# Linear attention and a leaky-ReLU MLP: the state's update in one VectorE operation, the decayed k in a tile of its own, another order of the first units, two raw weight buffers

## The chip, the cores and the metric

The kernel runs on one core of a Trainium2 chip. The metric is the device time of one execution in microseconds (us). Before the change the median of three runs is 626.47 us (625.44 to 629.3).

TensorE multiplies matrices into PSUM. VectorE (DVE in the profile), ScalarE (ACT) and GpSimd (POOL) work element by element; the SP engine only issues transfers here. Each engine works off its own instructions in order, and waits where an instruction needs another engine's result.

## What is computed

For 4 batches, 8 heads, 768 positions and 64 channels per head, an attention with decay goes through blocks of 64 positions and carries one 64x64 state per head. Its output is the input x of a two-layer network:

```python
for b in range(nb):                       # nb = 768 / 64 = 12 blocks
    intra = einsum('bhic,bhjc->bhij', qb, kb) * Dmask[None]
    intra = einsum('bhij,bhjd->bhid', intra, vb)
    inter = einsum('bhid,bhde->bhie', qb * lam_pow[None], kv_state)
    out[:, :, sl] = intra + inter
    kb_dec = kb * rev_pow[None]
    kv_state = lam_block * kv_state + einsum('bhsd,bhse->bhde', kb_dec, vb)
...
h = x @ w_in                              # x: 3072 x 512, w_in: 512 x 2048
g = maximum(0.01 * h, h)
return g @ w_out                          # w_out: 2048 x 512
```

The weights come as 64-bit floating-point numbers; everything else is 32-bit.

## The kernel before

**Chunks.** The attention is worked in 24 chunks of 128 positions, six per batch, each of two blocks. Chunk c has these stages:

- `load_kq`, `load_v`: five transfers on SP's queue into one of two sets of buffers `kqv`.
- `transposes`: four TensorE transposes of k (line 331, for the first four chunks into the PSUM bank named by `KT`, later into `po`) and four of q (into `pt`); then copies on ScalarE (lines 340, 341), the decay of k in place on GpSimd (line 345; VectorE is allowed for the first chunk, `KM`), and the scaled q on GpSimd (line 349, from the copy of q; for chunks below `QS` it would be VectorE, from PSUM).
- `scores`: the state products `kv` of decayed k and v, and the scores `go`, both on TensorE into the PSUM tile `psc` (line 286); then on VectorE the scores times the decay (line 375), and for each of the two blocks an addition of the state product to a state that has already been multiplied by the decay of a block (line 382, or a copy at a batch's start, line 380). After each block GpSimd writes the decayed state into the next of four state tiles (line 385), to which the next block adds.
- `outputs`: TensorE makes the output in `po` from scores and v (`own`) and from state and scaled q (`inter`, twice); ScalarE and VectorE split it into three fp32r terms xh, xl, xm (lines 430, 431, 433), the left operand of the network.

**Groups and units.** Four chunks make a group of 512 tokens, so there are six groups. `w_in` has eight weight pairs p of 256 columns. For each half of a pair, `to_float32` loads 512 KB into one of `NRAW` buffers `raw` (line 485, on ScalarE's queue; for the output weights line 488, on SP's), reads it three times with ScalarE (lines 497, 499, 501) and makes 32-bit numbers with VectorE (lines 503, 504). `parts` then splits the pair into wh, wl, wm (lines 510 or 512, 515, 521). `up(g, p, lo, hi)` is a unit: the product of group g's chunks lo to hi with pair p. For each of two column blocks f it has three products (h, l, m) of four matmuls each (line 561), ScalarE passes between them (lines 579, 582) and a store of the result to DRAM (line 585). Its PSUM banks `b10`, `b11`, `b2` go round; the first `EARLY` blocks leave out `b11`. A unit can be cut into pieces of fewer chunks, which then go as separate units.

**Down.** From 360 us on, `down` multiplies the stored results, split again into three terms, with `w_out` (line 620), whose weights pass through `raw` and DRAM during the groups before. The last `raw` buffer also holds the temporary `tt` of the final additions.

**The order.** `seq` at line 658 is a list written out by hand for groups 0 and 1: "a" is a whole chunk alone, "b" begins two chunks, "r" is a round (outputs of c, scores of c + 1, transposes of c + 2), "wi" a weight pair, "up" a unit. The class `Plan` collects all operations with an assumed engine and duration and the tiles they read and write. `emit` then lays them out, always taking what can start earliest, and among equals the lower place in `seq`; each engine's instructions are issued in that order. Where the plan expects TensorE to be idle, `busy` puts placeholder transposes (line 253) into a bank that is not used yet (`spare`); they end with the first unit that uses this bank.

```python
seq = [("a", 0), ("a", 1), ("a", 2), ("a", 3), ("wi", 1), ("b", 4), ("wi", 0), ("up", 0, 1), ("up", 0, 0), ("wi", 2),
```

The `att` tile holds all the attention's buffers (8608 words per partition); each `raw` buffer has 1024.

Of the kernel before, what the change touches and what calls it, by code (L numbers as in the profile page):

```python
# [36 lines left out]
class Plan:  # L37
# [2 lines left out]


    LAG = {"PE": 0.25, "ACT": 0.1, "DVE": 0.1, "POOL": 0.12, "DMA": 3.5}
    SOON = dict(LAG, DMA=2.0)

    def __init__(self):
        self.ops, self.last, self.rank = [], {}, 0.0
        self.chain, self.chains = None, {}
        self.warm = 0.0
        self.first = {"PE": 0.0, "ACT": 0.0, "DVE": 3.4, "POOL": 0.0, "DMA": 0.2}
        self.cold, self.idle, self.spare = 6.0, None, None  # L50

    def begin(self, name):
# [28 lines left out]
    def emit(self):  # L81
        n = len(self.ops)
        follows, heads = {}, {}
        for c in self.chains.values():
            m = [i for i in c if "PE" in self.ops[i][0]]
            for i in c[1:]:
                self.ops[m[0]][2].update(self.ops[i][2] - set(c))
            heads[m[0]] = m[1:]
            follows.update((i, m[0]) for i in m[1:])
        locked = []  # L90
        left = [len(o[2]) for o in self.ops]
        users = [[] for _ in range(n)]
        for i, o in enumerate(self.ops):
            for d in o[2]:
                users[d].append(i)
        free = dict(self.first)
        ends = [[] for _ in range(n)]
        able = {e: set() for e in free}
        for i, o in enumerate(self.ops):
            if not left[i]:  # L100
                for e in o[0]:
                    able[e].add(i)

        def since(i, e):
            return max((t + (0.0 if e == x != "DMA" else self.LAG[x]) for t, x in ends[i]), default=0.0)

        def good(i, e, t):
            ways = self.ops[i][0]
            return all(t + ways[e] <= max(free[x], t) + ways[x] + 0.3 for x in ways)

        done = []
        while len(done) < n:
            best = None
            for e in free:
                for i in able[e]:
                    if e == "PE" and (i != locked[0] if locked else i in follows):
                        continue
# [12 lines left out]
            if e == "PE" and t < self.cold:  # L130
                us *= 1.5
            elif e == "DVE" and fn is not None and free["POOL"] > t:
                us += 0.4 * min(free["POOL"] - t, us)
            free[e] = t + us
            done.append((t, len(done), i, e))
# [9 lines left out]
        soon.update(PE=self.warm, DVE=self.first["DVE"], DMA=self.first["DMA"])  # L145
        over = [(0.0, None)] * n
        for t, _, i, e in self.timeline:
            ways, fn, deps = self.ops[i][:3]
            t = max([soon[e]] + [over[d][0] + (0.0 if over[d][1] == e != "DMA" else self.SOON[over[d][1]]) for d in deps])
# [11 lines left out]
def kernel(  # L161
# [10 lines left out]
    nc = tc.nc  # L172
# [11 lines left out]
    T = GC * C  # L184
    WARM = 9
    LATER = 4.0
    KT, EARLY = "b11", 1
    QS = 0
    KM = 1
    NRAW = 3  # L190
    HALF = (slice(0, D), slice(D, 2 * D))
    assert D == 64 and KO == HP == 4 and SEQ % C == 0 and NCH % GC == 0 and d_model == T == 512 and NP % 4 == 0

# [29 lines left out]
    NA = 8608  # L223
    att = sb([P, NA], "att")
    used = 0

# [4 lines left out]
        return att[:, used - n:used]  # L231

    ident = part(P)
    kqv = [[part(H * D).rearrange("p (h d) -> p h d", h=H) for _ in range(2)] for _ in range(3)]
    kTs, qTs, qsTs = ([part(HP * C).rearrange("p (y t) -> p y t", y=HP) for _ in range(2)] for _ in range(3))
    sc = part(2 * HP * C2).rearrange("p (x y t) -> p x y t", x=2, y=HP)
# [13 lines left out]
    def busy(n):  # L250

        for _ in range(n):
            nc.tensor.transpose(out=b1[0][:, 0:P], in_=ident, identity=ident)  # L253

    busy(WARM)
    nc.gpsimd.memset(zero, 0.0)
    plan = Plan()
    plan.idle, plan.spare, plan.warm = busy, "b10", 1.3 + 0.22 * WARM
    add = plan.add

    def factors_k():
# [42 lines left out]
    def load_kq(c):  # L304
        b, n, i = of(c)
        for src, x, nm in ((k, 0, "k"), (q, 1, "q")):
            y, dst = src[b, :, n * C:(n + 1) * C, :], kqv[x][i]

            def go(y=y, dst=dst):
                for z in range(2):  # L310
                    nc.sync.dma_start(out=dst[:, z * HP:(z + 1) * HP, :], in_=y[z::2].rearrange("h p d -> p h d"))  # L311
            add("DMA", 1.15, go, [], [f"{nm}{i}"])

    def load_v(c):
        b, n, i = of(c)
        add("DMA", 1.15, lambda: nc.sync.dma_start(out=kqv[2][i], in_=v[b, :, n * C:(n + 1) * C, :].rearrange("h p d -> p h d")),
            [], [f"v{i}"])

    def transposes(c):
# [16 lines left out]
        def copies():  # L336
# [5 lines left out]
            kr = tk.rearrange("p (y x) d -> p y x d", x=2)  # L342
            nr = slice(0, C2 if n == NCB - 1 else P)
            add(*((("DVE", "POOL"), (0.7, 1.1)) if c < KM else ("POOL", 1.1)),
                lambda e="POOL": ENG[e].tensor_tensor(kr[nr], kr[nr], _bc(pow_k, 3, D)[nr], op=ALU.mult), ["fk"], [f"k{i}"])  # L345
            m = slice(1 if n == 0 else 0, 2)
            o, x = (z.rearrange("p y (t i) -> p y t i", t=2)[:, :, m, :] for z in (qsTs[i], pt if c < QS else qTs[i]))
            eng, e, us, dep = ("DVE", nc.vector, 0.7, "pt") if c < QS else ("POOL", nc.gpsimd, 1.2, f"qT{i}")
# [1 line left out]

        return copies

    def scores(c):
        b, n, i = of(c)
        tk, tv, kT, qT = kqv[0][i], kqv[2][i], kTs[i], qTs[i]
        n_pu = 1 if n == NCB - 1 else 2

        def go():
# [9 lines left out]
                        h = y // 2 + (2 * y + x) % HP * 2  # L368
                        quad(pu[t][:, y, :], t, tk[:, 2 * y + x, :], tv[:, h, :], x, start=y == 0)

        add("PE", 0.47, kv, [f"k{i}", f"v{i}"], ["psc"])
        add("PE", 0.47, go, [f"kT{i}", f"qT{i}"], ["psc"])

        def uses():
            add("DVE", 0.69, lambda: nc.vector.tensor_tensor(sc, psc[:, :, lower, :], decay, op=ALU.mult), ["psc", "fk"], ["sc"])  # L375
            for t in range(n_pu):
                j = 2 * c + t
                new = state[j % 4]
                if n == 0 and t == 0:
                    add("DVE", 0.42, lambda new=new: nc.vector.tensor_copy(new, pu[0]), ["psc"], [f"st{j % 4}"])  # L380
                else:
                    add("DVE", 0.42, lambda new=new, t=t: nc.vector.tensor_tensor(new, new, pu[t], op=ALU.add),  # L382
                        ["psc"], [f"st{j % 4}"])
                if n_pu == 2:
                    add("POOL", 0.7, lambda new=new, j=j: nc.gpsimd.tensor_tensor(state[(j + 1) % 4], new, _bc(lam_c, 2, D), op=ALU.mult),  # L385
                        [f"st{j % 4}", "fq"], [f"st{(j + 1) % 4}"])

        return uses

# [48 lines left out]
    def alone(c):  # L438
        load_kq(c)
        load_v(c)  # L440
        transposes(c)()
        scores(c)()
        outputs(c)()

    def begun(c):

        for x in (c, c + 1):
            load_kq(x)
            load_v(x)
            transposes(x)()  # L450
        scores(c)()

    def round_of(c):

# [11 lines left out]
        for x in after:  # L466
            x()
        if c + 2 < NCH:
            load_v(c + 2)


# [3 lines left out]
    def to_float32(kind, p, h, dst, key, after=()):  # L475
# [17 lines left out]
        def addend(dt, i):  # L493
            return low.bitcast(dt).rearrange("p (n two) -> p n two", two=2)[:, :, i]

        add("DMA", 1.6, load, after, [f"raw{j}"])
        add("ACT", 0.67, lambda: nc.scalar.activation(out=dst, in_=words(1, F32), func=AF.Abs, scale=2.0 ** -110),
            [f"raw{j}"], [key])
        add("ACT", 0.78, lambda: nc.scalar.activation(out=addend(U16, 0), in_=words(0, U32), func=AF.Copy, bias=0.0, scale=2.0 ** -29),
# [28 lines left out]
            to_float32("wi", p, h, w32[:, h, :], f"w32{h}")  # L528
        parts(p, w32f, ["w320", "w321"])

    ATT = ["fk", "fq", "sc"] + [f"{x}{i}" for x in ("k", "q", "v", "kT", "qT", "qsT") for i in range(2)] + [f"st{i}" for i in range(4)]
    NR = 4
    graw = [att[:, j * 2 * T:(j + 1) * 2 * T] for j in range(NR)]

# [73 lines left out]
    def down(g, p):  # L608

        nonlocal n_t  # L610
        for tb in range(GC):
# [43 lines left out]

    seq = [("a", 0), ("a", 1), ("a", 2), ("a", 3), ("wi", 1), ("b", 4), ("wi", 0), ("up", 0, 1), ("up", 0, 0), ("wi", 2),
# [77 lines left out]
```

## Time and profile before

| | us |
|---|---|
| median of three runs | 626.47 |
| the profiled execution's own time | 626.15 |
| its span | 623.6 |
| TensorE busy | 613.9 |
| its weight loads busy | 513.5 |
| VectorE busy | 297.9 |
| ScalarE busy | 281.2 |
| GpSimd busy | 91.7 |

The span is what the profile covers; 2.55 us of the execution lie around it. The page's second part cuts the span into 40 slices of 15.6 us; a digit is the busy share in tenths:

```profile
PE   8899999999999999999999999999999999999997
DVE  4799882400344333333145763735545454535531
ACT  3688875443577766664444722312222222314111
POOL 4852513300332222222000000000000000000000
DMA  9998844632787778842455762432524333333201
```

One reads a column from top to bottom: which engines were busy at the same time. In the list of groups, a row gives line, engine, operation, output and inputs with their shapes, how often, then the total busy us, the mean ns of one, and the idle time of the engine just before them with what ended it. In the timeline a row gives the start, the length, the engine and the line.

### The profile page before, as it was taken

The page shows a single profiled execution, that of the slowest core. Times are in us where ns is not written, and L with a number is a line of the kernel's source. Part 1 is how long each engine was busy: PE and PEld are TensorE (multiplying, and loading weights), DVE is VectorE, ACT ScalarE, POOL GpSimd, SP SyncE. Part 2 cuts the span into 40 slices and gives each one's busy share as a digit, 9 for nine tenths or more (in the row PEclk, how much of TensorE's full clock was granted, in tenths as well). Part 3 has the DMA queues.
Part 4 walks back from the last instruction along what each step waited for, and adds up shares of the span by engine and source line. Part 5 has one row for each costly group of instructions (what it writes and reads, how often), then busy time and mean ns, then how long its engine had stood idle before and what let it go on. Part 6 is the DMA issues. An engine that isn't in the chain of part 4 may idle for free.

```text
span 623.6 us, 13157 instructions
## 1 busy us (share of the span) xinstructions
PE 613.9 (98%) x5578; PEld 513.5 (82%) x5578; DVE 297.9 (48%) x366; ACT 281.2 (45%) x461; POOL 91.7 (15%) x95
## 2 busy tenths in 40 slices
PE   8899999999999999999999999999999999999997
PEld 7688888898888888888788888888888888888885
DVE  4799882400344333333145763735545454535531
ACT  3688875443577766664444722312222222314111
POOL 4852513300332222222000000000000000000000
PEclk9999999999999999999999999999999999999999
DMA  9998844632787778842455762432524333333201
GB/s 201 250 259 259 243 156 136 155 111 91 206 248 253 245 238 259 247 163 87 169 202 189 247 203 72 153 117 82 188 67 135 136 106 131 128 109 118 85 0 67
DMA packets 103706, 101.51 MB, mean 163 GB/s; under 512 B 78560, under 2 KB 80608, under 8 KB 103648
## 3 DMA queue, kind: packets, MB, share of 16 engines
q1 hardware_dynamic: 99152, 92.29, 47.3%
q10 hardware_dynamic: 4496, 8.39, 4.3%
q8 instruction: 43, 0.70, 0.5%
q14 instruction: 15, 0.12, 0.1%
HBM read 65.02 MB, written 35.65 MB: 161 GB/s over the span
## 4 chain that ended last, share of the span: by engine, by line
PE 96%; DMA 2%; SPq 0%; POOL 0%; DVE 0%; ACT 0%; issue 0%; DVEq 0%
PE b L561 43%; PE b L620 17%; PE po L620 11%; PE psc L620 10%; PE po L286 4%; PE pt L620 3%; PE psc L286 3%; PE po L331 2%; PE pt L331 2%; DMA att<-in_q_dram 2%; PE b L253 1%; DMA att<-in_k_dram 1%; SPq L311 0%; PE b L331 0%; POOL att L345 0%
## 5 line engine op out<-in xcount | busy, mean ns | idle before, releaser
L602 ACT ACTIVATE xh<-att 128x1024 fp32r<-128x1024 f32 x48 | 50.9, 1061 | 147.3 <-PE po L620 141.3
L603 DVE SCALAR_TENSOR_TENSOR xl<-att,xh 128x1024 fp32r<-128x1024 f32 x48 | 58.7, 1223 | 99.4 <-ACT xh L602 99.4
L561 PE MATMUL b<-xh,wh 128*128 128x512 f32 (+3 forms) x416 | 105.5, 377 | 0.0
L561 PE MATMUL b<-xl,wl 128*128 128x512 f32 (+3 forms) x416 | 105.4, 376 | 0.0
L561 PE MATMUL b<-xm,wm 128*128 128x512 f32 (+3 forms) x416 | 104.9, 381 | 0.0
L561 PEld LDWEIGHTS b<-xl,wl 128*128 128x128 f32 x416 | 75.5, 188 | 14.7 <-DVE wl L515 0.2
L561 PEld LDWEIGHTS b<-xh,wh 128*128 128x128 f32 x416 | 75.3, 188 | 14.3
L561 PEld LDWEIGHTS b<-xm,wm 128*128 128x128 f32 x416 | 73.5, 188 | 13.2
L579 ACT ACTIVATE b<-b 128x512 f32<-128x512 f32 (+2 forms) x98 | 56.7, 579 | 57.1 <-PE b L561 56.3
L582 ACT ACTIVATE gs<-b 128x512 f32<-128x512 f32 (+2 forms) x98 | 57.8, 590 | 48.7 <-PE b L561 40.2
L375 DVE TENSOR_TENSOR att<-psc,att 128x512 f32<-128x512 f32 x24 | 16.5, 688 | 128.3 <-PE psc L286 128.2
L620 PE MATMUL b<-wl,xl 128*128 128x512 f32 x192 | 74.7, 389 | 0.0
L620 PE MATMUL b<-wh,xh 128*128 128x512 f32 x192 | 74.7, 389 | 0.0
L605 DVE SCALAR_TENSOR_TENSOR xm<-xl,xh 128x1024 fp32r<-128x1024 f32 x48 | 58.8, 1226 | 4.8
L345 POOL TENSOR_TENSOR att<-att 128x512 f32<-128x512 f32 (+1 forms) x24 | 27.6, 1149 | 141.1 <-PE po L331 133.5
L620 PEld LDWEIGHTS b<-wh,xh 128*128 128x128 f32 x192 | 36.1, 188 | 7.5
L620 PEld LDWEIGHTS b<-wl,xl 128*128 128x128 f32 x192 | 36.0, 188 | 7.5
L385 POOL TENSOR_TENSOR att<-att 128x256 f32<-128x256 f32 x40 | 35.6, 889 | 28.7 <-DVE att L382 23.4
L620 PE MATMUL po<-wm,xm 128*128 128x512 f32 (+1 forms) x100 | 37.2, 381 | 0.7 <-ACT raw L642 0.7
L620 PE MATMUL psc<-wh,xh 128*128 128x512 f32 x96 | 37.4, 389 | 0.0
L620 PE MATMUL po<-wl,xl 128*128 128x512 f32 x96 | 37.4, 389 | 0.0
L620 PE MATMUL b<-wm,xm 128*128 128x512 f32 x96 | 37.4, 389 | 0.0
(67 smaller groups left out, 817.1 us busy)
## 6 DMA issues: line engine op xcount, KB each, us to landing
att<-g SPq DMA_DIRECT2D x48, 512.0 KB, 3.2
g<-gs SPq DMA_DIRECT2D x45, 512.0 KB, 2.9
raw<-in_moe_w_in_dram ACTq DMA_DIRECT2D x16, 512.0 KB, 5.0
raw<-in_moe_w_out_dram SPq DMA_DIRECT2D x16, 512.0 KB, 4.3
att<-in_k_dram SPq DMA_DIRECT2D x48, 128.0 KB, 4.0
att<-in_q_dram SPq DMA_DIRECT2D x48, 128.0 KB, 3.7
att<-in_v_dram SPq DMA_DIRECT2D x24, 256.0 KB, 3.9
out_dram<-gs SPq DMA_DIRECT2D x23, 256.0 KB, 2.2
```

Source lines behind the costliest of these rows:

```text
L286: nc.tensor.matmul(dst[HALF[cols]], lhsT=lhsT[HALF[rows]], rhs=rhs[HALF[rows]], start=start, stop=True, skip_group_check=True)
L331: nc.tensor.transpose(out=at[y], in_=src[:, 2 * y:2 * y + 2, :].rearrange("p a d -> p (a d)"), identity=ident)
L345: lambda e="POOL": ENG[e].tensor_tensor(kr[nr], kr[nr], _bc(pow_k, 3, D)[nr], op=ALU.mult), ["fk"], [f"k{i}"])
L375: add("DVE", 0.69, lambda: nc.vector.tensor_tensor(sc, psc[:, :, lower, :], decay, op=ALU.mult), ["psc", "fk"], ["sc"])
L385: add("POOL", 0.7, lambda new=new, j=j: nc.gpsimd.tensor_tensor(state[(j + 1) % 4], new, _bc(lam_c, 2, D), op=ALU.mult), [f"st{j % 4}", "f ...
L561: nc.tensor.matmul(dst, lhsT=w[z][:, kk * 2 * P + f * P:kk * 2 * P + (f + 1) * P], rhs=x[z][:, kk, toks], start=start and kk == 0, stop=kk ...
L579: add("ACT", ns, lambda b=b: nc.scalar.activation(out=b, in_=b, func=AF.Copy, bias=0.0, scale=S + 1.0), [], [kb], rank=-1.5)
L582: add("ACT", ns, lambda b=b, r=r: nc.scalar.activation(out=r, in_=b, func=AF.Prelu, bias=0.0, scale=1.0 / WS, alpha=0.01), [kb], [f"gs{jg} ...
L602: add("ACT", 1.05, lambda: nc.scalar.activation(out=h, in_=graw[j], func=AF.Copy, bias=0.0, scale=NEAR), reads, wr("h"))
L603: add("DVE", 1.25, lambda: nc.vector.scalar_tensor_tensor(l, graw[j], 1.0, h.bitcast(F32), op0=ALU.mult, op1=ALU.subtract), reads + [f"rh{ ...
L605: add("DVE", 1.25, lambda: nc.vector.scalar_tensor_tensor(m, l.bitcast(F32), -S, h.bitcast(F32), op0=ALU.mult, op1=ALU.add), [f"rh{j}", f" ...
L620: nc.tensor.matmul(acc[tb][z // 2][:, cols], lhsT=ring[j][z][:, f * T + tb * P:f * T + (tb + 1) * P], rhs=W[pp][z][:, f * d_model:(f + 1) ...
```

## The change

- **State.** The GpSimd product at line 385 and the addition at line 382 are replaced by `scalar_tensor_tensor` on VectorE: new state = old state times the decay, plus the state product from PSUM. The factor is one number per partition and head pair, so an update is four instructions of 128x64.
- **Decayed k.** It goes into a tile `k_dec` of its own, one for all chunks, in a new stage `decayed(c)`, which the units "a", "b" and "r" call; the state products read `k_dec`.
- **Order.** `seq` for groups 0 and 1 is another list. Pair 1 comes after chunk 1, pair 0 after chunk 3; units cut into pieces are now 1 and 2 of group 0 (two halves each) and 7 of group 1 (three chunks and one).
- **Banks.** k's first transposes use `b10`, placeholders `b11`, and two early blocks leave out `b11`. The scaled q of chunks 0 and 1 is VectorE's, from PSUM (`QS` = 2).
- **Buffers.** `raw` has two buffers in place of three; `att` grows by 512 words.
- **Planning.** The plan names the loads of `w_in` an engine "WDMA" of its own, which it lets share time with "DMA", and some assumed durations differ. These add no instruction.

```diff
-    KT, EARLY = "b11", 1
-    QS = 0
+    KT, EARLY = "b10", 2
+    SPARE = "b11" if KT == "b10" else "b10"
+    QS = 2
     KM = 1
-    NRAW = 3
+    NRAW = 2
...
+    k_dec = part(H * D).rearrange("p (h d) -> p h d", h=H)
...
-            nc.tensor.transpose(out=b1[0][:, 0:P], in_=ident, identity=ident)
+            nc.tensor.transpose(out=bank[SPARE][:, 0:P], in_=ident, identity=ident)
...
-            add(*((("DVE", "POOL"), (0.7, 1.1)) if c < KM else ("POOL", 1.1)),
-                lambda e="POOL": ENG[e].tensor_tensor(kr[nr], kr[nr], _bc(pow_k, 3, D)[nr], op=ALU.mult), ["fk"], [f"k{i}"])
...
+    def decayed(c):
+        b, n, i = of(c)
+        nr = slice(0, C2 if n == NCB - 1 else P)
+        kr, kd = (z.rearrange("p (y x) d -> p y x d", x=2)[nr] for z in (kqv[0][i], k_dec))
+        add(*((("DVE", "POOL"), (0.7, 1.1)) if c < KM else ("POOL", 1.1)),
+            lambda e="POOL": ENG[e].tensor_tensor(kd, kr, _bc(pow_k, 3, D)[nr], op=ALU.mult), ["fk", f"k{i}"], ["kd"])
...
-        add("PE", 0.47, kv, [f"k{i}", f"v{i}"], ["psc"])
+        add("PE", 0.47, kv, ["kd", f"v{i}"], ["psc"])
...
-                new = state[j % 4]
+                new, old = state[j % 4], state[(j - 1) % 4]
+
+                def update(new=new, old=old, t=t):
+                    for y in range(HP):
+                        nc.vector.scalar_tensor_tensor(new[:, y, :], old[:, y, :], lam_c[:, y:y + 1], pu[t][:, y, :],
+                                                       op0=ALU.mult, op1=ALU.add)
...
-                    add("DVE", 0.42, lambda new=new, t=t: nc.vector.tensor_tensor(new, new, pu[t], op=ALU.add),
-                        ["psc"], [f"st{j % 4}"])
-                if n_pu == 2:
-                    add("POOL", 0.7, lambda new=new, j=j: nc.gpsimd.tensor_tensor(state[(j + 1) % 4], new, _bc(lam_c, 2, D), op=ALU.mult),
-                        [f"st{j % 4}", "fq"], [f"st{(j + 1) % 4}"])
+                    add("DVE", 0.55, update, ["psc", "fq", f"st{(j - 1) % 4}"], [f"st{j % 4}"])
...
         transposes(c)()
+        decayed(c)
         scores(c)()
...
+        decayed(c)
         scores(c)()
+        decayed(c + 1)
...
         if c + 2 < NCH:
+            decayed(c + 2)
             load_v(c + 2)
...
-        add("DMA", 1.6, load, after, [f"raw{j}"])
+        add("WDMA" if kind == "wi" else "DMA", 1.65, load, after, [f"raw{j}"])
...
-    seq = [("a", 0), ("a", 1), ("a", 2), ("a", 3), ("wi", 1), ("b", 4), ("wi", 0), ("up", 0, 1), ("up", 0, 0), ("wi", 2),
-           ("r", 4), ("wi", 3), ("up", 0, 2), ("up", 0, 3), ("r", 5), ("r", 6), ("r", 7), ("wi", 7), ("up", 1, 3, 0, 1),
-           ("wi", 4), ("up", 1, 1, 0, 2), ("wi", 6), ("up", 0, 7), ("up", 0, 4), ("up", 1, 7, 1, 3), ("up", 0, 6),
-           ("wi", 5), ("up", 0, 5), ("up", 1, 5), ("r", 8), ("r", 9), ("r", 10), ("up", 1, 7, 3, 4), ("r", 11),
-           ("up", 1, 2), ("up", 1, 0), ("up", 1, 7, 0, 1), ("up", 1, 3, 1, 4), ("up", 1, 1, 2, 4), ("up", 1, 6),
-           ("up", 1, 4)]
+    seq = [("a", 0), ("a", 1), ("wi", 1), ("a", 2), ("a", 3), ("wi", 0), ("up", 0, 1, 0, 2), ("b", 4), ("wi", 2), ("r", 4),
+           ("wi", 3), ("up", 0, 0), ("up", 0, 1, 2, 4), ("up", 0, 2, 0, 2), ("up", 0, 2, 2, 4), ("up", 0, 3), ("r", 5),
+           ("wi", 7), ("wi", 6), ("up", 0, 7), ("r", 6), ("up", 1, 7, 0, 3), ("up", 0, 6), ("wi", 4), ("r", 7), ("wi", 5),
+           ("up", 0, 4), ("up", 1, 6), ("up", 0, 5), ("r", 8), ("up", 1, 3), ("r", 9), ("up", 1, 5), ("up", 1, 7, 3, 4),
+           ("r", 10), ("up", 1, 0), ("r", 11), ("up", 1, 4), ("up", 1, 2), ("up", 1, 1)]
```

More of the change, by code (lines that the diff above doesn't have):

```diff
@@ L42 @@
     LAG = {"PE": 0.25, "ACT": 0.1, "DVE": 0.1, "POOL": 0.12, "DMA": 3.5}
-    SOON = dict(LAG, DMA=2.0)
+    LAG["WDMA"] = LAG["DMA"]
+    SOON = dict(LAG, DMA=2.0, WDMA=2.0)
+    LOADS = ("DMA", "WDMA")
     def __init__(self):
@@ L48, in __init__ @@
         self.warm = 0.0
-        self.first = {"PE": 0.0, "ACT": 0.0, "DVE": 3.4, "POOL": 0.0, "DMA": 0.2}
+        self.first = {"PE": 0.0, "ACT": 0.0, "DVE": 3.4, "POOL": 0.0, "DMA": 0.2, "WDMA": 0.2}
         self.cold, self.idle, self.spare = 6.0, None, None
@@ L104, in since @@
         def since(i, e):
-            return max((t + (0.0 if e == x != "DMA" else self.LAG[x]) for t, x in ends[i]), default=0.0)
+            return max((t + (0.0 if e == x and x not in self.LOADS else self.LAG[x]) for t, x in ends[i]), default=0.0)
         def good(i, e, t):
@@ L134, in emit @@
             free[e] = t + us
+            if e in self.LOADS:
+                free.update(dict.fromkeys(self.LOADS, t + us))
             done.append((t, len(done), i, e))
@@ L144, in emit @@
         soon = dict.fromkeys(free, 0.0)
-        soon.update(PE=self.warm, DVE=self.first["DVE"], DMA=self.first["DMA"])
+        soon.update(self.first, PE=self.warm)
         over = [(0.0, None)] * n
@@ L148, in emit @@
             ways, fn, deps = self.ops[i][:3]
-            t = max([soon[e]] + [over[d][0] + (0.0 if over[d][1] == e != "DMA" else self.SOON[over[d][1]]) for d in deps])
+            t = max([soon[e]] + [over[d][0] + (0.0 if over[d][1] == e and e not in self.LOADS else self.SOON[over[d][1]]) for d in deps])
             if e == "PE":
@@ L220 @@
     G = [[dram.tile([P, 2 * T], F32, name=f"g{g}_{p}", tag=f"g{g}_{p}") for p in range(NP)] for g in range(NG)]
-    NA = 8608
+    NA = 8608 + 512
     att = sb([P, NA], "att")
@@ L257 @@
     plan = Plan()
-    plan.idle, plan.spare, plan.warm = busy, "b10", 1.3 + 0.22 * WARM
+    plan.idle, plan.spare, plan.warm = busy, SPARE, 1.3 + 0.22 * WARM
     add = plan.add
@@ L311, in go @@
                     nc.sync.dma_start(out=dst[:, z * HP:(z + 1) * HP, :], in_=y[z::2].rearrange("h p d -> p h d"))
-            add("DMA", 1.15, go, [], [f"{nm}{i}"])
+            add("DMA", 1.2, go, [], [f"{nm}{i}"])
     def load_v(c):
         b, n, i = of(c)
-        add("DMA", 1.15, lambda: nc.sync.dma_start(out=kqv[2][i], in_=v[b, :, n * C:(n + 1) * C, :].rearrange("h p d -> p h d")),
+        add("DMA", 1.2, lambda: nc.sync.dma_start(out=kqv[2][i], in_=v[b, :, n * C:(n + 1) * C, :].rearrange("h p d -> p h d")),
             [], [f"v{i}"])
@@ L341, in copies @@
             add("ACT", 0.6, lambda: nc.scalar.copy(qTs[i], pt), ["pt"], [f"qT{i}"])
-            kr = tk.rearrange("p (y x) d -> p y x d", x=2)
-            nr = slice(0, C2 if n == NCB - 1 else P)
-            add(*((("DVE", "POOL"), (0.7, 1.1)) if c < KM else ("POOL", 1.1)),
-                lambda e="POOL": ENG[e].tensor_tensor(kr[nr], kr[nr], _bc(pow_k, 3, D)[nr], op=ALU.mult), ["fk"], [f"k{i}"])
             m = slice(1 if n == 0 else 0, 2)
@@ L351, in transposes @@
         return copies
+    def decayed(c):
[4 more added lines that the diff above has]
+            lambda e="POOL": ENG[e].tensor_tensor(kd, kr, _bc(pow_k, 3, D)[nr], op=ALU.mult), ["fk", f"k{i}"], ["kd"])
     def scores(c):
         b, n, i = of(c)
-        tk, tv, kT, qT = kqv[0][i], kqv[2][i], kTs[i], qTs[i]
+        tk, tv, kT, qT = k_dec, kqv[2][i], kTs[i], qTs[i]
         n_pu = 1 if n == NCB - 1 else 2
@@ L529, in w_in @@
         parts(p, w32f, ["w320", "w321"])
-    ATT = ["fk", "fq", "sc"] + [f"{x}{i}" for x in ("k", "q", "v", "kT", "qT", "qsT") for i in range(2)] + [f"st{i}" for i in range(4)]
+    ATT = ["fk", "fq", "sc", "kd"] + [f"{x}{i}" for x in ("k", "q", "v", "kT", "qT", "qsT") for i in range(2)] + [f"st{i}" for i in range(4)]
     NR = 4
```

## The prediction

> **What bounds the kernel now.** I read the busy shares first, then the chain of waits, then the busy times by stretch, then the timeline of the first 70 us. TensorE is busy 98% of the span and its weight loads 82%; the chain that ended last is TensorE almost throughout:
>
> ```profile
> PE 96%; DMA 2%; SPq 0%; POOL 0%; DVE 0%; ACT 0%; issue 0%; DVEq 0%
> ```
>
> So an edit counts only where it removes work from TensorE or closes a hole in it. The stretches show where holes are; the columns after the length are TensorE matmuls, its weight loads, VectorE, ScalarE and GpSimd, each in busy us, then the clock, the DMA share and GB/s:
>
> ```profile
> 0.00:30.00 30.00, 24.92 (x576) 20.07 (x577) 18.37 (x42) 15.63 (x28) 18.72 (x24) 1.00 0.99 224
> 30.00:60.00 30.00, 30.00 (x426) 24.93 (x425) 28.43 (x37) 25.58 (x45) 11.87 (x11) 1.00 0.93 264
> 60.00:90.00 30.00, 30.00 (x394) 26.56 (x394) 25.75 (x38) 24.59 (x44) 11.65 (x10) 1.00 0.71 210
> 125.00:310.00 185.00, 184.72 (x2180) 155.82 (x2180) 55.60 (x89) 111.49 (x204) 38.01 (x40) 1.00 0.60 192
> ```
>
> Only the first 30 us have holes: 5.1 us idle, and beside it the placeholder transposes of line 253, which compute nothing. From 30 us on TensorE has none; but VectorE is busy 28.43 of 30 us between 30 and 60, so it is nearly a second bound there. From 125 us VectorE is 30% busy. Groups of instructions and one line of the waits (us in total, times, longest):
>
> ```profile
> L253 PE MATMUL b<-att 128*128 128x128 f32 x38 | 8.4, 349 | 1.4 <-POOL att L256 1.4
> L382 DVE TENSOR_TENSOR att<-att,psc 128x256 f32<-128x256 f32 x40 | 16.5, 412 | 5.0 <-POOL att L385 5.0
> L385 POOL TENSOR_TENSOR att<-att 128x256 f32<-128x256 f32 x40 | 35.6, 889 | 28.7 <-DVE att L382 23.4 <-DVE att L380 4.7 <-DMA att<-in_k_dram 0.5
> DVE att L382 <- POOL att L385: 5.0, 5, 2.2
> ```
>
> TensorE's removable start is thus at most 5.1 + 8.4 = 13.5 us; some 4 us of it, until the first k lands at 4.0, no order of the units touches. The timeline gives the dates that matter (start, length, engine):
>
> ```profile
> 10.00 0.38 ACTq L485 DMA_DIRECT2D raw<-in_moe_w_in_dram  x1
> ...
> 14.61 0.37 ACTq L485 DMA_DIRECT2D raw<-in_moe_w_in_dram  x1
> ...
> 26.27 1.22 DVE L515 SCALAR_TENSOR_TENSOR wl<-wh,w 128x1024 fp32r<-128x1024 f32 x1
> ...
> 29.46 2.12 PE L561 MATMUL b<-xh,wh 128*128 128x512 f32 x8
> ```
>
> The two halves of the first weight pair are asked for at 10.0 and 14.6, and the first weight product runs at 29.46. Later pairs come just in time: the l part of pair 2 is made at 45.60 to 46.83 while TensorE starts that unit at 46.01, that of pair 3 at 53.96 to 56.27 for a unit begun at 54.68. VectorE, in order, makes them.
>
> [...] Trace: line 512 takes 1.44 us at 35.28 beside GpSimd's line 345, 0.69 alone; line 382, one input in PSUM, never left 0.40 to 0.42. The new update has one SBUF tensor and one PSUM tensor, so I expect it undisturbed.
>
> **Part by part.**
>
> *State update.* Removed: 40 GpSimd products (35.6 us), and 40 VectorE additions of 412 ns. Added: 160 scalar_tensor_tensor of 128x64. No row shows that size. Line 649, the same operation from PSUM, takes 692 ns at 512 columns and 420 at 256: 1.06 ns a column, so 216 ns at 64. Neighbours overlap: line 375 (0.69 us) starts at 13.48 and its follower at 14.07, line 382 (0.41) at 14.07 and its follower at 14.40, so 0.08 us of each is hidden. Four: 4 x 0.136 + 0.08 = 0.62 us (lower end), or 4 x 0.216 = 0.86 without overlap (upper end). I take 0.62: +0.21 per update, +8.4 us on VectorE in all; the cover after 125 us is its 70% idle. Up to pair 7 (some 65 us) about 13 updates matter: +2.7 us, at the upper end +5.9. Gained there: VectorE waits for line 385 before 60 us (1.24, 0.51, 0.51 and 0.52 at 11.7, 23.6, 28.0, 39.3) = 2.8 us; and weight operations stretched beside line 385 (0.85 for 0.42 at 40.8, similar at 16.3, 22.1, 60.2) about 1.5 us of 10. The additions at 17.2 and 24.1, which hold back the next scores on TensorE by 0.7 and 0.3 us, come sooner too.
>
> *Decayed k.* Same GpSimd product (1.06 us), new target, no longer waiting for the k transposes, but for the previous chunk's state products; a k load no longer waits for these (SP's wait of line 311 on psc, 7.4 us) but for the decay. Queued behind the waiting decay on GpSimd is the scaled q of the next chunk. The decay has a whole round, 7.5 us or more, until its user: nothing on the path. If that cover is gone, 1.1 us per early chunk. Range -1 to +1 us; I take 0.
>
> *Scaled q of chunks 0 and 1 on VectorE from PSUM:* +0.42 and +0.69 us while VectorE is largely idle (7.3 to 12.9 us); saves 0.6 + 1.28 on the chain through ScalarE and GpSimd. Counted in the start.
>
> *Order.* Pair 1 moves ahead of chunks 2 and 3, pair 0 ahead of chunks 4 and 5. What moves per pair: two issues of 0.37 us on ScalarE's queue, past the kT and qT copies there; 1 MB, some 4.2 us of DMA at 250 GB/s, which k, q and v of the next two chunks now follow on SP's queue; six ScalarE passes (0.67 + 0.78 + 0.78 twice = 4.5 us); on VectorE 2 x (0.42 + 0.69) + 0.69 + 1.22 + 1.22 = 5.4 us, ahead of the later chunks' additions. GpSimd issues nothing of it. With halves asked for near 7 and 10 us and 5 us to land, both are read by 17.5, and the first product can run near 21 instead of 29.5. That is the upper bound of the start's gain; products must also exist to fill it, and pair 0 (landed near 25, ready near 31) gates the next unit: some 6.5 us at most.
>
> But the gain lasts only as far as VectorE follows. The old order put before pair 7's unit two pieces of group 1 (one chunk of pair 3, two of pair 1): 6 x 0.42 + 6 x 0.48 = 5.4 us of TensorE work that the new order moves behind it. Pair 7's l part was ready at 65.70 and used at 68.76: 3.1 us slack. VectorE is earlier by 3 us (work pulled into its 11.6 idle us of the first 30; my choice, 0 to 6 possible) + 2.8 + 1.5 - 2.7 = 4.6. So the start may shrink by 3.1 + 4.6 - 5.4 = 2.3 us; I take **2.0**.
>
> *Fewer pieces.* A product of four matmuls takes 0.91 us at 512 columns, 0.48 at 256 and 0.39 to 0.45 at 128 (starts 66.87 to 67.35, 58.37 to 58.76, 60.13 to 60.58), and 384 lies near 0.70. A unit has six. Cut in two halves it costs 6 x (0.96 - 0.91) = 0.3 us more, cut 3 to 1 6 x 0.21 = 1.26, cut 1-2-1 6 x 0.41 = 2.5. Before: one of each, 4.0. After: two halved and one 3 to 1, 1.9. TensorE saves **2.2** us, for certain if nothing waits.
>
> *Two raw buffers.* A buffer's cycle is 0.37 + 5.0 to land + reads that spread over 3.0 us (31.38 to 34.45) = 8.4, so 4.2 per half with two; before, halves were asked for every (77.9 - 10.0)/15 = 4.5 us. It fits by 0.3. The loads of the output weights lie some 28 us apart and are covered. Range 0 to +6; I take 0. The altered planning numbers add no instruction.
>
> Sum: -2.2 - 2.0 = -4.2 us. Profiled run: span 623.6 to 619.4, with the 2.55 around it 626.15 to 622.0. The median, 626.47, lies 0.3 higher: **622.3**.
>
> **Rivals.**
> - *The whole start* (chance 0.20): VectorE keeps up, since its idle time takes 6 or more us; -6.5 - 2.2 gives 617.8. For: the 11.6 idle us. Against: 28.43 of 30.
> - *VectorE becomes the bound at pair 7* (0.12): TensorE waits there 5.4 - 3.1 + L, with L VectorE's lateness against before; minus 2.2 saved. Slower from L above -0.1. With updates at the upper end, L = 5.9 and no credits: wait 8.2, +6.0, 632.5. Against: two of the credits are visible waits.
> - *Two buffers starve* (0.13): landings of 6.6 us, the longest seen, add 0.8 per half over 8 halves less the slack of 2.4, and evictions queue behind ScalarE's waiting read: +4, so 626.3. For: ScalarE waited for raw twice (1.1 us) even with three.
> - *The order does not bring pair 1 forward* (0.10): its issue sits on ScalarE's in-order queue behind copies that wait for TensorE; only the pieces gain, 624.3.
>
> **How the numbers follow.** The forecast has 0.45, with a range of its own of 620 to 625. 1% is 6.3 us, about what a measurement of this kernel can tell. Under 620.2: most of the first rival and the forecast's edge, 0.24. Over 632.7: the upper half of the second and an edge of the third, 0.07. The range from 617.5 to 628.5 leaves out the tail of the first and most of the second rival.
>
> **What would show it.** Right: first weight product near 21 us, placeholders under 5 us, no line 385, update groups of about 0.14 us a step, TensorE without holes from 35 us; pieces of 128 columns down to a third. Wrong: TensorE waiting for line 515 near 60 us (second rival), ScalarE for raw over 3 us (third), first product after 27 us (fourth).

## The result, and the profile after

The changed kernel takes 631.53 us (median of 12 runs, 629.18 to 632.94) against 626.52 us. Over all runs the ratio is 1.0066, 95% interval 1.0047 to 1.0084, so it is 4.1 us slower (the medians alone are 5.0 us apart), measurably but by less than 1%. The forecast was 4.2 us faster. The clock granted to TensorE explains little of it: the two profiled executions had 0.999 and 1.000 and took 630.1 and 626.15 us, 3.95 us apart. In this section and the next, line numbers are those of the changed kernel where nothing else is said: 259 for 253, 292 for 286, 337 for 331, 351 for 349, 360 for 345, 384 for 375, 391 for 382, 425 for 414, 442 for 431, 512 for 497, 527 for 512 (so 512 is now one of ScalarE's reads of `raw`), 530 for 515, 576 for 561.

The same stretches as before, with the same columns (length; TensorE, its weight loads, VectorE, ScalarE, GpSimd busy; clock, DMA share, GB/s):

```profile
0.00:30.00 30.00, 22.64 (x520) 18.78 (x521) 22.67 (x59) 14.62 (x26) 9.73 (x14) 1.00 0.97 219
30.00:60.00 30.00, 26.41 (x505) 23.75 (x504) 28.52 (x47) 21.91 (x39) 10.01 (x7) 1.00 0.84 228
60.00:90.00 30.00, 28.25 (x356) 23.89 (x355) 25.29 (x42) 24.31 (x44) 5.96 (x5) 1.00 0.82 228
125.00:310.00 185.00, 184.54 (x2278) 154.65 (x2274) 60.30 (x157) 111.99 (x205) 27.21 (x24) 1.00 0.60 191
```

One reads the second column. TensorE now stands still for 7.4 us in the first stretch (5.1 before), 3.6 in the second and 1.8 in the third (0 before); from 125 us to the end it is 5.2 against 4.7. The groups that answer to those shown of before, and last the row of before that L527 answers to:

```profile
L259 PE MATMUL b<-att 128*128 128x128 f32 x35 | 6.8, 320 | 1.4 <-POOL att L262 1.4
L391 DVE SCALAR_TENSOR_TENSOR att<-att,psc 128x64 f32<-128x64 f32 x160 | 33.1, 274 | 0.6 <-DVE att L395 0.5
L527 DVE TENSOR_SCALAR wh<-w 128x1024 fp32r<-128x1024 f32 x7 | 9.8, 1393 | 0.2
L512 DVE TENSOR_SCALAR wh<-w 128x1024 fp32r<-128x1024 f32 x7 | 6.8, 971 | 0.2
```

Idle time of the first 90 us and placeholders together were 5.1 + 8.4 = 13.5 us and are 12.7 + 6.8 = 19.5: 6.0 us lost. The rest of TensorE's work shrank from 613.9 - 8.4 to 610.4 - 6.8 us, by 1.9, which agrees with the fewer pieces, whose durations in the prediction hold (four matmuls of 256 columns start at 50.37 and the next four at 50.85; of 128 at 121.19 and 121.58). With the 0.5 us of idle time after 125 us this is, but for rounding, the 4.7 us by which the two spans differ (628.3 and 623.6). The four longest waits of TensorE in the first 125 us (us, times, longest):

```profile
PE b L576 <- DVE wh L527: 2.7, 1, 2.7
PE po L292 <- ACT att L425: 2.1, 2, 1.9
PE po L292 <- DVE att L384: 1.6, 2, 1.0
PE b L576 <- DVE wl L530: 1.4, 2, 1.1
```

The longest wait is for wh of pair 0. In the timeline (start, length, engine) of VectorE, of GpSimd and of TensorE around it one sees why:

```profile
33.60 3.90 DVE L527 TENSOR_SCALAR wh<-w 128x1024 fp32r<-128x1024 f32 x1
37.42 0.68 DVE L442 TENSOR_TENSOR xl<-po,xh 128x512 fp32r<-128x512 f32 x1
```

```profile
33.31 1.17 POOL L360 TENSOR_TENSOR att<-att 64x512 f32<-64x512 f32 x1 [3.73 <-PE psc L292]
34.45 2.50 POOL L351 TENSOR_TENSOR att<-att 128x512 f32<-128x512 f32 x2
```

```profile
34.16 0.74 PE L576 MATMUL b<-xh,wh 128*128 128x256 f32 x4
37.56 1.19 PE L576 MATMUL b<-xh,wh 128*128 128x512 f32 x4 [2.66 <-DVE wh L527]
38.59 0.60 PE L337 MATMUL po<-att 128*128 128x128 f32 x4
```

An instruction of 0.69 us takes 3.90: it began 0.3 us after the first of three GpSimd products that follow each other without a pause, and ended 0.5 us after the last. TensorE, in order, stands at the first product of the unit of pair 0. Behind it in TensorE's order are the transposes of a k (38.59) and the second product of pair 1's second piece (39.95). They weren't ready either: both need the xl of chunk 3 (37.42), which stands behind wh on VectorE, the product as its operand and the transposes because it still reads the `po` that they write.

In the kernel before, the same wh of pair 0 was held up too, to 1.44 us, but TensorE had other work until it was ready; and a later wh of the changed kernel waited for one GpSimd product only:

```profile
35.28 1.44 DVE L512 TENSOR_SCALAR wh<-w 128x1024 fp32r<-128x1024 f32 x1
37.44 1.98 PE L561 MATMUL b<-xh,wh 128*128 128x512 f32 x8
```

```profile
66.67 1.43 DVE L527 TENSOR_SCALAR wh<-w 128x1024 fp32r<-128x1024 f32 x1
68.13 2.21 DVE L530 SCALAR_TENSOR_TENSOR wl<-wh,w 128x1024 fp32r<-128x1024 f32 x1
```

```profile
70.40 1.19 PE L576 MATMUL b<-xl,wl 128*128 128x512 f32 x4 [1.06 <-DVE wl L530]
```

At 66.67 the next GpSimd product followed without a pause, and it was the one to last longer (1.75 us; most products of line 351 take 1.29). Why wh at 33.60 waited through all three is not shown. The weights at 66.67 and 68.13 are those of pair 7; its wl, stretched by 1.0 us beside that GpSimd product, makes TensorE wait 1.06 us in the middle of the unit, the fourth wait of the list.

The start went as forecast in its date and not in its worth. The first weight product runs at 22.13 in place of 29.46 (the forecast said 21), yet the first 30 us hold no less lost time: 5.1 + 8.4 = 13.5 before, 7.4 + 6.3 = 13.7 now. The scores of chunk 3 moved from 24.11 to 27.66. The first half of pair 1, asked for at 8.18, is read at 14.41, after 6.2 us:

```profile
14.41 0.66 ACT L512 ACTIVATE w<-raw 128x512 f32<-128x512 f32 x1 [2.71 <-DMA raw<-in_moe_w_in_dram]
...
16.22 0.13 ACT L425 COPY att<-po 128x2 f32<-128x2 f32 x1
```

ScalarE waits 2.71 us for it, and behind the three reads stands the tiny copy that TensorE needs to go on with chunk 1's output: the wait of 1.9 us in the list above.

### The profile page after: what moved, and what is told of

It is laid out like the page before. It is cut to its first block, busy times and chain, and to the rows that moved or that the text cites. A ratio compares the mean times of both kernels' runs of the same rounds, so it can differ in the third digit from the quotient of the medians.

```text
span 628.3 us, 13190 instructions
## 1 busy us (share of the span) xinstructions
PE 610.4 (97%) x5551; PEld 509.9 (81%) x5551; DVE 310.4 (49%) x487; ACT 281.0 (45%) x460; POOL 57.6 (9%) x53
## 4 chain that ended last, share of the span: by engine, by line
PE 89%; DVE 7%; DMA 2%; issue 1%; SPq 1%; ACT 0%; DVEq 0%; ACTq 0%
PE b L576 39%; PE b L635 17%; PE po L635 10%; PE psc L635 10%; PE pt L635 3%; PE po L292 3%; PE psc L292 3%; PE po L337 2%; DVE wh L527 1%; DMA raw<-in_moe_w_in_dram 1%; DVE wl L530 1%; PE pt L337 1%; DVE w L519 1%; DVE att L391 1%; DMA att<-in_q_dram 1%
## 5 line engine op out<-in xcount | busy, mean ns | idle before, releaser
L597 ACT ACTIVATE gs<-b 128x512 f32<-128x512 f32 (+2 forms) x97 | 57.6, 594 | 50.2 <-PE b L576 40.8
L360 POOL TENSOR_TENSOR att<-att 128x512 f32<-128x512 f32 (+1 forms) x24 | 26.1, 1089 | 167.7 <-PE psc L292 123.8
L292 PE MATMUL po<-att 64*64 64x64 f32 x1472 | 33.4, 222 | 5.3 <-ACT att L425 2.4
L292 PEld LDWEIGHTS po<-att 64*64 64x64 f32 x1472 | 27.6, 134 | 13.1 <-issue 6.4
L635 PE MATMUL psc<-wl,xl 128*128 128x512 f32 x96 | 37.3, 389 | 0.0
```

What stands on the lines that cost most here:

```text
L292: nc.tensor.matmul(dst[HALF[cols]], lhsT=lhsT[HALF[rows]], rhs=rhs[HALF[rows]], start=start, stop=True, skip_group_check=True)
L360: lambda e="POOL": ENG[e].tensor_tensor(kd, kr, _bc(pow_k, 3, D)[nr], op=ALU.mult), ["fk", f"k{i}"], ["kd"])
L597: add("ACT", ns, lambda b=b, r=r: nc.scalar.activation(out=r, in_=b, func=AF.Prelu, bias=0.0, scale=1.0 / WS, alpha=0.01), [kb], [f"gs{jg} ...
L635: nc.tensor.matmul(acc[tb][z // 2][:, cols], lhsT=ring[j][z][:, f * T + tb * P:f * T + (tb + 1) * P], rhs=W[pp][z][:, f * d_model:(f + 1) ...
```

## The experiments

Theories: **V**, VectorE is late because the update is long; **G**, because GpSimd's products hold it up; **O**, the new order is at fault by itself; **R**, two raw buffers are too few. All runs, as ratios to the kernel before on the same chip:

| run | ratio | 95% interval |
|---|---|---|
| the changed kernel | 1.0066 | 1.0047 to 1.0084 |
| old_order | 1.0106 | 1.0078 to 1.0133 |
| old_update | 1.0068 | 1.0043 to 1.0093 |
| plan_true_update | 1.0068 | 1.0053 to 1.0083 |
| after_three_raw | 1.0054 | 1.0039 to 1.0069 |
| before_new_update | 1.0023 | 1.0014 to 1.0032 |
| before_new_order | 1.0018 | 1.0008 to 1.0029 |
| before_two_raw | 1.0030 | 1.0020 to 1.0040 |
| before_own_k | 1.0048 | 1.0032 to 1.0065 |
| before_banks_q | 1.0048 | 1.0029 to 1.0067 |
| cheap_update | 1.0004 | 0.9987 to 1.0021 |
| no_gpsimd_reads | 0.9977 | 0.9966 to 0.9987 |
| three_products_out | 1.0018 | 1.0007 to 1.0029 |
| both_relieved | 0.9972 | 0.9959 to 0.9985 |
| before_no_gpsimd_reads | 1.0001 | 0.9986 to 1.0016 |
| before_slow_add | 1.0013 | 1.0001 to 1.0026 |
| half_scaling | 1.0009 | 0.9999 to 1.0019 |
| products_after_wh | 1.0050 | 1.0029 to 1.0070 |
| products_after_wh_three_raw | 1.0012 | 1.0004 to 1.0019 |

### Parts of the change, alone or undone

One part of the change undone in the changed kernel, or one part alone in the kernel before.

```diff
# old_order: the list "seq" of the kernel before, in the changed kernel
# before_new_order: the list of the changed kernel, in the kernel before
# old_update / before_new_update: the same exchange for the update of the state
# before_two_raw (kernel before)
-    NRAW = 3
+    NRAW = 2
# after_three_raw (changed kernel)
-    NRAW = 2
+    NRAW = 3
# plan_true_update (changed kernel)
-                    add("DVE", 0.55, update, ...
+                    add("DVE", 0.86, update, ...
```

> The changed kernel with the order list of before (all else as changed: update on VectorE, k_dec, two raw buffers, banks). Theory O, the new order of the first units costs the time: near or under before, 622 to 627 us, holes of TensorE in the first 90 us back to 13 us with its placeholders. Theory V, the updates make VectorE late whatever the order: 630 to 634 us, since the old order also has VectorE 95% busy from 30 to 60 us.

> The changed kernel with the old state update (GpSimd scales, VectorE adds), everything else as changed. Theory V: 625 to 628 us, as VectorE gets 0.45 us per update back. Theory O: 630 to 633 us. If GpSimd's extra two-input operations stall VectorE more than the updates cost it: above 633 us.

> The kernel before with two raw buffers in place of three, nothing else. Theory R, two buffers starve ScalarE: 629 to 632 us, ScalarE waiting for raw over 3 us. Otherwise 626 to 627 us.

> The kernel before with the new update on VectorE alone (decayed k in place, old order, three raw buffers). Theory V: 629 to 631 us. Theory O: 625 to 627 us, with GpSimd relieved.

> The kernel before with the new order list alone (old update, decayed k in place, three raw buffers, old banks). Theory O: 630 to 634 us. Theory V: 622 to 626 us, as the list saves 2.2 us of pieces and VectorE has its old load.

> The changed kernel with the plan told 0.86 us for an update in place of 0.55, the duration the trace shows. The plan may then issue other things first. Theory V: 627 to 630 us. Theories O and G: 630 to 633 us, no systematic change.

> The changed kernel with three raw buffers in place of two, nothing else. Theory R, the third buffer is part of the loss (before lost 1.6 us without it): 629 to 630 us. If VectorE's lateness covers the loads: 631 to 632 us.

The two parts not covered by these, the own tile for the decayed k (stage `decayed`, `k_dec`) and the banks with the scaled q on VectorE (`KT`, `EARLY`, `SPARE`, `QS`), were put into the kernel before by themselves.

> The kernel before with the decayed k in a tile of its own, alone (old update, old order, three raw buffers). The parts measured alone so far (update +1.7, order +1.4, raw +1.6 us) sum to 4.7 us, about the whole loss; if the parts add up, this one is 0: 626 to 626.5 us. If k loads that no longer wait for the state products help: 624 to 625.5 us.

> The kernel before with the change's banks (k's transposes in b10, placeholders in b11, two early blocks) and the scaled q of chunks 0 and 1 on VectorE, alone. If the parts add up: 626 to 627 us. If the shorter chain of the first chunks counts by itself: 624.5 to 625.5 us.

Each of the five parts alone makes the kernel before slower, by 0.18 to 0.48%. Their sum, 0.23 + 0.18 + 0.30 + 0.48 + 0.48 = 1.67%, is two and a half times the whole. Nor does undoing the order or the update in the changed kernel help: 1.0106 and 1.0068. So these runs don't tell what a part costs. The plan lays out all instructions anew after every edit, and a list of units that was put together for one set of durations leaves holes with another. The expectation that the parts would add up, formed after the first of these runs, was wrong. So was the hope that a plan with the true duration of the update would find a better order. What can be said: neither list is at home in the other kernel, and no single part is the culprit.

### The same order on every engine

The second kind of run keeps every engine's order and changes only how long an operation takes.

```diff
# cheap_update (changed kernel)
-                    for y in range(HP):
-                        nc.vector.scalar_tensor_tensor(new[:, y, :], old[:, y, :], lam_c[:, y:y + 1], pu[t][:, y, :],
-                                                       op0=ALU.mult, op1=ALU.add)
+                    nc.vector.scalar_tensor_tensor(new, old, lam_c[:, 0:1], pu[t], op0=ALU.mult, op1=ALU.add)
# no_gpsimd_reads (changed kernel), before_no_gpsimd_reads; three_products_out for c == 5 (k), c in (4, 5) (q)
-   ENG[e].tensor_tensor(kd, kr, _bc(pow_k, 3, D)[nr], op=ALU.mult)
+   nc.gpsimd.memset(kd, 0.5)
-   e.tensor_tensor(o, x, _bc(pow_q, 2, 2)[:, :, m, :], op=ALU.mult)
+   nc.gpsimd.memset(o, 0.5)
# before_slow_add (kernel before)
-   nc.vector.tensor_tensor(new, new, pu[t], op=ALU.add)
+   [nc.vector.tensor_tensor(new[:, y, :], new[:, y, :], pu[t][:, y, :], op=ALU.add) for y in range(HP)]
```

> The changed kernel, the same instructions in the same order, but an update is one scalar_tensor_tensor of 128x256 with the factor of the first head pair for all of them (the other factors are left out). Its time should be 0.41 in place of 0.86 us. Theory V: 625 to 628 us. Theory O or contention with GpSimd: 630 to 632 us, as the big waits (2.7 us for wh, 1.9 us for the copy behind the raw read) have other causes.

> The changed kernel, the same order, but GpSimd's decayed k and scaled q are written by a memset (the two products are left out), which reads nothing and is short. Theory G, [...]: 626 to 628 us, the 3.9 us wh at 33.6 back to 0.7 and the 2.7 us hole of TensorE gone. Theories V and O: 630 to 631.5 us.

> The kernel before, every engine's order kept, the decayed k and scaled q written by a memset on GpSimd (the products are left out; the scaling of the state stays). If the contention is new with the change: 625 to 626.5 us. If the kernel before pays it as well: 619 to 622 us.

> The changed kernel, every engine's order kept, with a memset for three GpSimd products only, those from 33.3 to 37.0 us in its profile: the decayed k of chunk 5 and the scaled q of chunks 4 and 5 (left out). If the one stall of wh is a loss of its own: 628.5 to 629.5 us, wh at 0.7 in place of 3.9 us. If VectorE is late all the same and other waits take its place: 630.5 to 631.5 us.

> The changed kernel, every engine's order kept, with both the update of 128x256 with one factor and GpSimd's products left out. If update and contention are two separate losses: 619 to 621 us. If they fill the same holes: 622 to 624.5 us, the forecast's 622.3 among it.

> The kernel before, every engine's order kept, the addition of the state as four of 128x64 in place of one of 128x256 (0.86 in place of 0.41 us expected; same result, GpSimd unchanged). Theory V, the update's duration itself costs: 629 to 632 us. If only the changed kernel's order is sensitive to it, or any other layout costs 1 to 3 us whatever is edited: 626 to 627.5 us.

**GpSimd.** Without GpSimd's reads the changed kernel gains 0.89% (5.6 us), the kernel before nothing (1.0001). So the contention with these products became a cost with the change, and all the loss can come from it. In neither kernel's profile does TensorE wait for one of these products themselves, which speaks against the memset's shorter time as the cause. (The scaling of the state, which only the kernel before has, stayed in.) The second result says more. VectorE's row in the kernel before without these reads, from 30 to 60 us (length, VectorE busy, clock, DMA share, GB/s):

```profile
30.00:60.00 30.00, 25.30 (x40) 1.00 0.92 258
```

VectorE has 3.1 us less to do there than the 28.43 of before, and the kernel is no faster. A new wait at the start hides little: TensorE waits 2.3 us longer for k there, but the first weight product comes at 29.06 (29.46 before). Busy for 95% of a stretch, VectorE still wasn't a bound.

**The one stall.** Three products out of 46 (the rest of GpSimd's as in the changed kernel) take 0.48% (3.0 us) off, three quarters of the loss. The timeline of that run, VectorE and then TensorE:

```profile
33.52 1.70 DVE L527 TENSOR_SCALAR wh<-w 128x1024 fp32r<-128x1024 f32 x1
```

```profile
35.27 1.19 PE L576 MATMUL b<-xh,wh 128*128 128x512 f32 x4 [0.46 <-DVE wh L527]
```

The wait for wh falls from 2.66 to 0.46 us. Even a memset, which only writes, holds wh up by 1.0 us; the expectation of 0.7 us missed that.

**The update.** At 0.48 us (the mean of cheap_update's 128x256 operations in the first 125 us) in place of 0.86 the changed kernel gains 0.62% (3.9 us). But both relieved together give 0.9972, no more than GpSimd alone (0.9977): update and contention fill the same holes. In cheap_update wh runs at 32.04 and takes 0.69 us, ahead of GpSimd's products. A shorter update moved it out of their way; the wl after it then took 3.20 us. So the 3.9 us are for the most part not the price of 40 updates but of being late at one place: with the long updates left in, three_products_out gets 3.0 us of them.

In the kernel before, four additions per update cost 0.13%, 0.8 us. This run also measures what I had estimated. The groups of the two kernels, first before_slow_add, then, for comparison, the row of line 391 above:

```profile
L382 DVE TENSOR_TENSOR att<-att,psc 128x64 f32<-128x64 f32 x160 | 24.3, 213 | 4.8 <-POOL att L385 4.8
```

```profile
11.36 0.61 DVE L382 TENSOR_TENSOR att<-att,psc 128x64 f32<-128x64 f32 x4 [1.25 <-POOL att L385]
```

Four additions of 128x64 take 0.61 us, my estimate for the update. The update with a factor per partition takes 0.86: 274 ns for one in place of 213. The expectation of 0.86 for the additions was wrong, so this run tests a smaller burden than it meant to.

### Variants

Two more ideas: the kernel before with half of GpSimd's scaling of the state, and the changed kernel with the three products placed behind wh.

```diff
# half_scaling (kernel before), from chunk 1 on
+   t == 0: nc.vector.tensor_tensor(new, old, pu[0], op=ALU.add)              # k of block 0 carries 1 / factor
+           nc.gpsimd.tensor_tensor(state[(j + 1) % 4], new, factor of two blocks)
+   t == 1: nc.vector.tensor_tensor(new, new, pu[1], op=ALU.add)              # no scaling after it
# products_after_wh (changed kernel); with three raw buffers also NRAW = 3
-   ["fk", f"k{i}"], ["kd"])
+   ["fk", f"k{i}"] + (["wh0"] if c == 5 else []), ["kd"])
-   ["fq", dep], [f"qsT{i}"])
+   ["fq", dep] + (["wh0"] if c in (4, 5) else []), [f"qsT{i}"])
```

> A variant of the kernel before that leaves half of GpSimd's state products out without giving VectorE more work: from chunk 1 on, the decayed k of a chunk's first block carries the inverse factor of a block and the scaled q of its second block the factor, so the first update is an addition of 128x256 (0.41 us) to the state as it is, and GpSimd scales once per chunk, by the factor of two blocks. Same result. If contention with GpSimd (7 us in the changed kernel) and the wait of the additions for it cost the kernel before too: 622 to 625.5 us. If VectorE's load alone decides: 626 to 627 us.

In this kernel the inverse factors stand in another order of the heads than the k they multiply, so it does not compute the same result; the instructions and their sizes are those described, with a few small operations of VectorE more at the start, and the plan lays them out anew. With half of GpSimd's scaling gone it is no faster (1.0009), which agrees with before_no_gpsimd_reads: in the kernel before, GpSimd isn't in the way.

> The changed kernel; the decayed k of chunk 5 and the scaled q of chunks 4 and 5 wait for the wh of pair 0, so GpSimd computes them behind it. Same result; the order of the other engines stays but for some operations near 40 us. If the stall of wh is what costs: 627.5 to 629 us, wh at 0.7 us and no wait of TensorE for it over 1 us. If VectorE is late all the same: 630.5 to 632 us.

> The same with three raw buffers. If the raw buffer's 0.8 us is a loss of its own: 627 to 628 us. If both fill the same holes: as the run with two buffers.

With three raw buffers, 1.0054 becomes 1.0012, and the intervals are apart: 2.6 us for three products moved behind one instruction, in a kernel that computes everything. With two buffers, 1.0066 becomes 1.0050, which the intervals don't tell apart, though its profile has wh at 0.69 us and TensorE waiting 0.2 us for it; there TensorE stands 4.1 us, 2.7 at once, for nothing that the profile shows. The 2.7 us fall in the middle of a row of sixteen 64x64 products: five had run, and the sixth waits for no other engine. The profiled execution was also the slowest of its eight (631.9 us, median 628.92), so whether the others have this pause is not shown. Once the stall is gone, the third buffer, with the new layout that it brings, is worth 0.38%. No variant that computes the whole result beat the kernel before.

## Why the prediction was wrong

- **What bounds the kernel.** TensorE does, and an edit counts where it makes or closes a hole: right, the holes account for the loss. That VectorE "is nearly a second bound" from 30 to 60 us was read from 28.43 busy of 30 us and from units that begin as their weights are ready. The runs showed otherwise: 3.1 us less work for it there changed nothing. Part of that busy time was waiting for GpSimd (28.43 us with the k and q products, 25.30 without), and weights made just in time need not be made late.
- **The step that failed** is the sum "VectorE is earlier by 3 us + 2.8 + 1.5 - 2.7 = 4.6". At pair 7, which it speaks of, VectorE was 4.6 us later instead: the l part was ready at 70.34, before at 65.70. Its third term had the wrong sign. I counted contention as a mean that falls with GpSimd's load (35.6 us less). What matters is whether a weight operation meets products in a row just where TensorE has nothing else in front of it. GpSimd's busy time fell from 91.7 to 57.6 us, and yet the seven wh took 9.8 us in place of 6.8, and the price of the contention with the k and q products rose from 0 to 5.6 us. The prediction had pair 0 "ready near 31": its wh was ready at 37.50, and 3.2 us of this delay are the stall. The start's lost time did not shrink by 2.0 us but grew by 6.0.
- **The update** was sized at 0.62 us and is 0.86, the upper end that I gave. That GpSimd leaves it undisturbed was right: all 160 took 266 to 281 ns, the 12 of them beside a GpSimd instruction 270 to 281. The row I worked from, line 649 of before, has a fixed number as its factor, not one per partition. The step of 0.136 us that I took from one start to the next fits plain additions (0.13: four in 0.61 us in before_slow_add), not line 391: 0.19, eight in 1.61 us from 13.03 on.
- **The order**: the first weight product at 22.13 was right, the gain of 2.0 us was not. I had named that k, q and v then follow 1 MB of weights (an estimate of 4.2 us from the GB/s of the trace), and did not subtract it: chunk 3's scores came 3.6 us later (24.11 to 27.66). I gave the load 5 us to land; it took 6.2.
- **VectorE beside GpSimd.** The stretched wh that I went by took 1.44 us for 0.69, at 35.28 of before. The wh at 66.67 of the changed kernel was like it, 1.43 us, and waited for one product; the one at 33.60 took 3.90 and waited through three.
- **Fewer pieces**: priced right, 1.9 us measured for 2.2.
- **Two raw buffers**, taken as 0 within 0 to 6: alone they cost the kernel before 0.30%, though ScalarE waited no longer for `raw` (1.2 us against 1.1), so the layout is in this too; in the changed kernel their share shows only once the stall is gone (0.38%).
- **The own k tile**, 0 within -1 to +1: alone it cost 0.48%, but through a new layout; its own price stays open.
- **The rivals.** The second had the right mechanism, VectorE late at a weight pair, and in part the right place: pair 7's unit, begun at 68.24, waits 1.06 us for its l part (line 530, 515 of before). The larger wait, 2.7 us, is at pair 0 at 34 us. The third rival's sign came true, ScalarE waited 3.4 us for `raw`, but 2.7 of it were for the first half of pair 1, whose buffer was free; with three buffers, in products_after_wh_three_raw, that wait was 2.8. The second rival's -0.1 us as the point where it decides was too exact for a sum with an estimate in each term. Measured, 631.5 lies beyond the upper end of the range, 628.5.

What stays open: how much of the quarter of the loss beyond the stall belongs to the wait at pair 7, to the raw buffers, to the displaced loads or to the layout; why wh waited through three products at 33.60; and what TensorE waits for where the profile shows no releaser.

## What to carry to other kernels

An engine that is busy for 95% of a stretch need not bound it: take work from it with every order kept, and look whether the time moves. Where a planner or a hand-made list sets the order, undoing one part of a change measures the part and the new layout together; change durations and keep the order instead. When an in-order engine gets a new task list, look on both sides of a long wait: here one late wh on VectorE held TensorE, and the xl that TensorE's next work needed stood behind wh.

## What the runs showed of the hardware

- One VectorE operation, the wh of pair 0 (0.69 us by itself), took 3.90 us in the changed kernel, behind three GpSimd products that follow each other without a pause, 1.70 in three_products_out, behind three memsets, and 0.69 in products_after_wh, where the products come after it. It need not wait through all of them: at 66.67 in the changed kernel the same operation took 1.43 us, behind one product, and the next product took 1.75 (most of that line take 1.29). Which of the two happens is not explained by these runs.
- At 128x64, scalar_tensor_tensor from PSUM with a factor per partition took 274 ns (line 391 of the changed kernel; 0.19 us from start to start), a plain tensor_tensor 213 ns (line 382 of before_slow_add; 0.13).
- The factor per partition: at 128x256 scalar_tensor_tensor took 475 ns with it in cheap_update and 420 ns with a fixed number (line 649 of the kernel before), a plain addition 412 ns (line 382 of the kernel before). At 128x64 there is no run with a fixed number, so the 61 ns there hold the operation and the factor together. Four small updates (0.86 us in the changed kernel) cost nearly twice one large one.
- The update, with one operand from SBUF and one from PSUM, was not held up by GpSimd in the changed kernel: 266 to 281 ns in 160 instructions, 270 to 281 in the 12 beside a GpSimd instruction.
